# Attention and two dense layers on one core: one PSUM bank for the weighted values, seven common banks, and a new order from corrected durations

## The chip, the cores and the metric

The kernel runs on one core of a Trainium2 chip. Its engines are TensorE (PE, with its weight loads as PEld), VectorE (DVE), ScalarE (ACT), GpSimd (POOL) and SyncE (SP), which issues most transfers; each works through its own queue in order. TensorE writes into PSUM, which has eight banks here; DVE and ACT read it. The metric is the device time of one execution in microseconds: 618.28 us, median of three runs (617.89 to 619.36).

## What is computed

Inputs are q, k, v of shape (2, 8, 1152, 64) and the weights of two dense layers, all in 64-bit words that the kernel turns into pairs of 32-bit numbers (high and low part).

```python
q_pool = q.reshape(B, H, S // 2, 2, D).mean(axis=3)          # 576 queries a head
scores = scale * np.matmul(q_pool, k.transpose(0, 1, 3, 2))
scores = scores - np.max(scores, axis=-1, keepdims=True)
attn = np.exp(scores)
attn = attn / (np.sum(attn, axis=-1, keepdims=True) + 1e-09)
attn_out = np.matmul(attn, v)                                # as (1152, 512)
h = x @ w_in;  g = np.maximum(h, 0.0) + np.log1p(np.exp(-np.abs(h)));  x = g @ w_out
h = np.maximum(np.maximum(x @ w1, x @ w2), x @ w3);  out = h @ w_out2
```

## The kernel before

Two heads make a pair; there are eight pairs, and a pair's 576 queries are cut into units: three for pair 0 (128, 224 and 224 queries wide), two of 288 for each other pair, 17 units in all (`UNIT`). The keys come in nine tiles of 128. For a pair, q and k are loaded, transposed (`turn_q`, `turn_k`, the tiles `tq`, `tk`) and split into a high and a low part (`high_q`, `low_k`, ...). A first pass (`scores`, tile `s`, L908) multiplies the high parts alone, and DVE takes maxima from it (`part_max`, L921), which `spread` (tile `tm`) brings to all partitions.

A unit's main work is then, for each key tile j: `turned` (L956) makes transposed scores `st` from three products of high and low parts for two heads, into two banks; `exps` (L966) on ACT turns each into `p`; `add_p` (L975), on POOL, sums `p` into `acc`. `values` (L983) multiplies `p` with v for three key tiles at a time into the bank `x` of the unit; `x_6_1` below means the second such group of unit 6, `st_7_4` key tile 4 of unit 7. After the last key tile `sum_up` (L997) makes the row sum `l` in a common bank, and a chain follows: `keep_sum` (L1004), `log_sum` (L1010), `near_inverse` (L1014) on ACT, `inverse` in two steps (L1020, L1022) and `divide` (L1028) on DVE, which reads the bank `x` and writes the result `xy`.

TensorE works in three forms: row-split (two matmuls of 64 rows beside each other: `st`, `s`), column-split (64 columns: `x`, `l`, `tm`) and whole (the transposes).

The order of all this is written by a list scheduler (`Order.ordered`) when the program is built: each piece of work has an engine, a duration, a place (a wished time) and what it reads and writes; the engine that is free first takes the piece with the smallest place among those that could start. A change of TensorE's form costs `CHANGE` in it and `stay` in the place. Most PSUM results take a bank out of a pool `s` of common banks and give it back when their last reader is through (`take`, `free`): six in the kernel before, and two more for `x`, odd and even units apart. The places come from the table `AK`.

The first nine weights of the dense layers are rebuilt at low priority in the attention part (`early_float`, L259 to L272, and `low_weight`, L292, on DVE, with a common bank each). Then the dense part runs (`project`, L1213 in `matmul3`), with all eight banks under new names; its first matmul waits for the last reader of the bank that it gets.

Of the kernel before, what the change touches and what calls it, by code (L numbers as in the profile page):

```python
# [8 lines left out]
F32 = mybir.dt.float32  # L9
# [7 lines left out]
P = 128  # L17
# [13 lines left out]
SB = 448  # L31
BANK = 512

AK = {"load": 18.806, "load1": -361.956, "q1": 465.624, "k1": -601.474, "v0": -174.412, "p1": 16.097, "p2": -1.542, "kl": 95.048, "c0": -340.25, "v": 83.029, "q": -26.274, "k": -25.681, "pass": 2.655, "gap": 2.142, "values": 111.836, "sum": 55.437, "stay": 33.792}
WINDOW = 25.652
NPT = 20
ON_DVE = ((), (8,))
VALUES = ((0, 1, 2), (3, 4, 5), (6, 7, 8))
GOOD = 128 * 2 * 17
# [13 lines left out]
class Order:  # L53
# [1 line left out]

    CHANGE = {"rows": 0.21, "columns": 0.11, "whole": 0.15}
    AFTER = {"PE": 0.30, "ACT": 0.22, "DVE": 0.20, "POOL": 0.22, "SP": 2.6, "AQ": 2.6}

    def __init__(self, **pools):
# [87 lines left out]
def kernel(  # L149
# [22 lines left out]
    NJ = S // P  # L172
# [24 lines left out]
    ps = inner.enter_context(tc.tile_pool(name="ps", bufs=1, space=PSUM, side="right"))  # L197
# [110 lines left out]
    if exact:  # L308
        order = Order(t=NTB)
        tiles = {}  # L310
# [8 lines left out]
        for n in range(2):  # L319
            q1 = st.tile([P, 2, NQ + TAILQ], F32R, tag=f"q1{n}", name=f"q1_{n}")  # L320
# [415 lines left out]
        for n in range(NPRE + 3):  # L736
# [5 lines left out]
            if n < NPRE:  # L742
                for step in range(3):
                    order.add("DVE", (0.42, 0.65, 0.65)[step], late + 2 + step, float_weight, n, step,
                              reads=(f"raw{n % 3}", f"size{n % 2}"), writes=(f"t{n % 2}",))
# [3 lines left out]
            _, _, _, f, args, *_ = order.work[n]  # L749
            f(*args)  # L750
    else:
        order = Order(s=6)
        TRIO = 0.41
        order.mode = dict.fromkeys(("scores", "turned"), "rows") | dict.fromkeys(("values", "sum_up", "spread"), "columns")
        order.stay = AK["stay"]
        order.AFTER = {"PE": 0.20, "ACT": 0.16, "DVE": 0.14, "POOL": 0.10, "SP": 2.6}
        tiles = {}
        HQ = NQ // 2
# [166 lines left out]
        def step_of(u):  # L925
            return [w for w in range(UNITS) if UNIT[w][0] == UNIT[u][0]].index(u)
# [49 lines left out]

        def values(u, js):
            if js[0] == 0:
                tiles["x", u] = ps.tile([P, HQ], F32, tag=f"x{u % 2}", name=f"x_{u}")
            x, (pr, _, W) = tiles["x", u], UNIT[u]  # L980
            for j in js:
                for i in range(2):
                    nc.tensor.matmul(  # L983
                        x[halves(i), :W],
                        tiles["v", pr][:, i, j],
                        tiles["p", u, j][:, i, :W],
                        start=(j == 0),
                        stop=(j == NJ - 1),
                    )
# [60 lines left out]
        def name_of(n):  # L1050
            return f"b{n[1]}"
# [6 lines left out]
        def prepare_first():  # L1058
# [4 lines left out]
            for g, (t0, t1) in enumerate(q_parts(0)):  # L1063
# [3 lines left out]
                order.add("ACT", (0.21, 0.5)[g], p, high_q, 0, g, n, reads=(name_of(n),), writes=(f"qh0{g}",) if g else ("qh00", "qh01"))  # L1067
                order.add("DVE", (0.22, 0.55)[g], AK["c0"], low_q, 0, g, n, reads=(name_of(n), f"qh0{g}"), writes=(f"ql0{g}",), free=n)
            for g in range(NB):
                n, p = next_bank(), -55 + g  # L1070
                order.add("PE", 0.4, p, turn_k, 0, g, n, reads=(f"k{g}",), writes=(name_of(n),), take=n)
                order.add("ACT", 0.38, p, high_k, 0, g, n, reads=(name_of(n),), writes=[f"kh0{h}" for h in range(g, NB if g == 0 else g + 1)])
                order.add("DVE", 0.475, p + AK["kl"], low_k, 0, g, n, reads=(name_of(n), f"kh0{g}"), writes=(f"kl0{g}",), free=n)
            order.add("SP", 2.8, AK["v0"], load_v, 0, reads=(f"kh0{NB - 1}",), writes=("v0",))

        def prepare(pr):
            at, y = WINDOW * pr, pr % 2
            loads = AK["load1"] if pr == 1 else at + AK["load"]
            order.add("SP", 3.0, loads, load_q, pr, writes=("q", "q0"))
            order.add("SP", 3.0, loads + 0.1, load_k, pr, writes=["k"] + [f"k{g}" for g in range(NB)])  # L1080
            order.add("SP", 3.0, at + AK["v"], load_v, pr, reads=("k",), writes=(f"v{y}",))
            order.add(ADD_Q, 2.1 if ADD_Q == "POOL" else 1.3, (AK["q1"] if pr == 1 else at + AK["q"]) - 0.2, add_q, pr, reads=("q",), writes=("qs", "qs0"))
            for g in range(2):
                n, p = next_bank(), (AK["q1"] if pr == 1 else at + AK["q"]) + 0.5 * g
                order.add("PE", (0.24, 0.28)[g], p, turn_q, pr, g, n, reads=("qs",), writes=(name_of(n), f"tq{y}"), take=n)
                order.add("ACT", (0.38, 0.24)[g], p, high_q, pr, g, n, reads=(name_of(n),), writes=(f"qh{y}{g}",) if g else (f"qh{y}0", f"qh{y}1"))
                order.add("DVE", (0.47, 0.28)[g], p, low_q, pr, g, n, reads=(name_of(n), f"qh{y}{g}"), writes=(f"ql{y}{g}",), free=n)
            for g in range(NB):
                n, p = next_bank(), (AK["k1"] if pr == 1 else at + AK["k"]) + 0.5 * g
                order.add("PE", 0.28, p, turn_k, pr, g, n, reads=("k",), writes=(name_of(n), f"tk{y}"), take=n)  # L1090
                order.add("ACT", 0.38, p, high_k, pr, g, n, reads=(name_of(n),), writes=[f"kh{y}{h}" for h in range(g, NB if g == 0 else g + 1)])
                order.add("DVE", 0.475, p + AK["kl"], low_k, pr, g, n, reads=(name_of(n), f"kh{y}{g}"), writes=(f"kl{y}{g}",), free=n)

# [26 lines left out]
        def one_unit(u):  # L1120
            pr, c0, W = UNIT[u]
            y, part = pr % 2, W / HQ
            at, gap = WINDOW * pr + c0 / NQ * WINDOW, WINDOW / 2 / NJ * part
            for j in range(NJ):
                p, m = at + gap * j, u * NJ + j
                ns = [next_bank() for _ in range(2)]
                parts = range(1 if pr == 0 and step_of(u) == 0 else 2)
                order.add("PE", TRIO * max(part, 0.78), p, turned, u, j, *ns,
                          reads=[f"tq{y}", f"tk{y}"] + [f"{x}{y}{g}" for x in ("qh", "ql") for g in parts] + [f"{x}{y}{j // KT}" for x in ("kh", "kl")] + [f"nm{y}_{step_of(u)}"],
                          writes=[name_of(n) for n in ns], take=tuple(ns))  # L1130
                for i, n in enumerate(ns):
                    order.add("ACT", 0.09 + 0.23 * part, p, exps, u, j, n, i, reads=(name_of(n), f"shift{y}_{step_of(u)}"),
                              writes=(f"p{m % NPT}",), free=n)
                if j and j not in DIRECT:
                    engine = "DVE" if j in (ON_DVE[u % 2] if u + 1 < UNITS else LAST) else "POOL"
                    order.add(engine, 1.5 * part if engine == "POOL" else 0.96 * part, p, add_p, u, j, engine,
                              reads=[f"p{m % NPT}"] + ([f"p{(m - 1) % NPT}"] if j == 1 else []), writes=(f"acc{u % 2}",))
            for js in VALUES:
                p = at + gap * js[-1] + AK["values"] * part
                order.add("PE", 0.475 * len(js) * part, p, values, u, js,  # L1140
                          reads=[f"p{(u * NJ + j) % NPT}" for j in js] + [f"v{y}"], writes=(f"x{u % 2}",))
            n, p = next_bank(), at + gap * NJ + AK["sum"] * part
            order.add("PE", (0.475 + 0.475 * len(DIRECT)) * part, p, sum_up, u, n,
                      reads=[f"acc{u % 2}"] + [f"p{(u * NJ + j) % NPT}" for j in DIRECT], writes=(name_of(n),), take=n)
            r, x = f"rr{u % 2}", f"x{u % 2}"
            order.add("ACT", 0.58, p - 3, keep_sum, u, n, reads=(name_of(n),), writes=(r,))
            order.add("ACT", 0.34, p - 3, log_sum, u, writes=(r,))
            order.add("ACT", 0.53, p - 3, near_inverse, u, writes=(r,))
            order.add("DVE", 0.39, p - 3, inverse, u, 0, n, reads=(r,), writes=(name_of(n),))
            order.add("DVE", 0.39, p - 3, inverse, u, 1, n, reads=(name_of(n),), writes=(r,), free=n)  # L1150
            order.add("DVE", 0.39, p - 3, divide, u, reads=(r, x), writes=(f"xy{u}",))
            if (u + 1 == UNITS or UNIT[u + 1][0] != pr) and pr < NC:
                mine = [f"xy{w}" for w in range(UNITS) if UNIT[w][0] == pr]
                order.add("ACT", 0.45, p + 5, high_x, 0, pr, reads=mine, writes=(f"xh{pr}",))
                order.add("POOL", 1.08, p + 5, low_x, 0, pr, reads=(f"xh{pr}",))
# [16 lines left out]
        for n in range(NPRE + 3):  # L1172
# [5 lines left out]
            if n < NPRE:  # L1178
                t = next_bank()
                for step in range(3):  # L1180
                    order.add("DVE", 0.62, late + 2 if step == 0 else -100, early_float, n, step, t,
                              reads=(f"raw{n % 3}", f"size{n % 2}"), writes=(name_of(t),), take=None if step else t)
# [364 lines left out]
```

## Time and profile before

| | |
|---|---|
| median of three runs | 618.28 us (617.89 to 619.36) |
| the profiled execution | 618.21 us, span 616.4 us |
| TensorE's granted clock | 0.998 of full speed |
| first dense matmul | 252.94 us |
| PE busy in the span | 600.3 us (97%) |
| DVE, ACT, POOL busy | 407.1, 349.6, 366.8 us |

Times in rows are microseconds from the start of the span. A timeline row joins instructions of one group that follow each other: its first start, the time to the last end, and the count. Matmuls overlap in the pipe, so what a group takes from TensorE is read from its start to the next group's start, not from its length. A wait in brackets names what ended it.

### The profile page before, as it was taken

What the parts mean: (1) busy time and instruction counts of PE and PEld (TensorE: products, weight loads), DVE (VectorE), ACT (ScalarE), POOL (GpSimd) and SP (SyncE); (2) the same over time, 40 slices, a digit from 0 to 9 for tenths busy, and PEclk for the clock granted to TensorE, in tenths of its full rate; (3) what the DMA queues carried; (4) which work ended last, traced back from release to release, by engine and by line L of the source; (5) the groups of instructions that cost most, each with busy time, mean ns of one, the idle gap of its engine ahead of it and who ended that gap; (6) DMA issues with size and microseconds to landing.
All of it is one profiled execution on the core that took longest, in us unless ns stands there. A gap on an engine that the chain in (4) does not pass through costs nothing.

```text
span 616.4 us, 10975 instructions
## 1 busy us (share of the span) xinstructions
PE 600.3 (97%) x4116; PEld 512.3 (83%) x4116; DVE 407.1 (66%) x753; ACT 349.6 (57%) x817; POOL 366.8 (60%) x310
## 2 busy tenths in 40 slices
PE   7999999999999999999999999999999999999995
PEld 5866576666666566799999999999999999999994
DVE  5577667576779995789887988977888822212121
ACT  2656677776777779776777676766644312102101
POOL 1485787878888888499877878897946200000000
PEclk9999999999999999999999999999999999999999
DMA  6512131407042321133333333332234001001001
GB/s 154 154 41 85 33 93 24 116 2 208 13 112 70 107 79 61 34 104 104 102 109 117 117 104 103 102 103 70 68 103 138 35 1 52 0 1 53 0 1 56
DMA packets 53295, 46.68 MB, mean 76 GB/s; under 512 B 20592, under 2 KB 47216, under 8 KB 53232
## 3 DMA queue, kind: packets, MB, share of 16 engines
q1 hardware_dynamic: 51408, 45.29, 24.9%
q10 hardware_dynamic: 1824, 0.59, 0.4%
q8 instruction: 34, 0.56, 0.4%
q14 instruction: 29, 0.24, 0.1%
HBM read 43.52 MB, written 2.36 MB: 74 GB/s over the span
## 4 chain that ended last, share of the span: by engine, by line
PE 89%; DVE 5%; ACT 2%; POOL 1%; issue 1%; DMA 1%; SPq 0%; ACTq 0%; DVEq 0%; POOLq 0%
PE bank_h_m L1213 18%; PE bank_y L1213 16%; PE bank_h L1213 14%; PE st L956 12%; PE x L983 11%; PE bank_o L1213 6%; PE s L908 5%; PE l L997 2%; PE tk L881 2%; DVE nh L921 1%; ACT p L966 1%; DMA k<-in_k_dram 1%; PE tm L941 1%; PE tq L851 1%; DVE t L259 1%
## 5 line engine op out<-in xcount | busy, mean ns | idle before, releaser
L966 ACT ACTIVATE p<-st,shift 128x288 f32<-128x288 f32 (+2 forms) x306 | 127.3, 489 | 60.6 <-PE st L956 56.5
L975 POOL TENSOR_TENSOR acc<-acc,p 128x576 f32<-128x576 f32 (+2 forms) x96 | 128.2, 1335 | 15.6 <-ACT p L966 9.0
L921 DVE TENSOR_REDUCE nh<-s 128x1 f32<-128x512 f32 (+5 forms) x180 | 105.5, 631 | 40.5 <-PE s L908 40.0
L1213 PE MATMUL bank_h_m<-x,wh 128*128 128x384 f32 x432 | 114.1, 337 | 0.0
L1213 PE MATMUL bank_h<-x,wh 128*128 128x384 f32 x384 | 105.8, 338 | 1.9 <-DVE rr L1022 1.4
L248 POOL TENSOR_SCALAR size<-size 128x512 f32<-128x512 f32 x56 | 84.0, 1504 | 18.2 <-ACT size L243 18.1
L983 PE MATMUL x<-p,v 128*64 128x288 f32 (+2 forms) x612 | 81.5, 402 | 0.0
L1213 PEld LDWEIGHTS bank_h_m<-x,wh 128*128 128x128 f32 x432 | 78.7, 188 | 0.7
L1213 PE MATMUL bank_h_m<-x,wl 128*128 128x384 f32 x216 | 72.8, 337 | 0.0
L1213 PEld LDWEIGHTS bank_h<-x,wh 128*128 128x128 f32 x384 | 70.3, 188 | 2.8 <-issue 1.8
L956 PE MATMUL st<-qh,kh 64*128 64x288 f32 (+2 forms) x306 | 65.4, 351 | 1.7 <-DVE nh L921 1.0
L1268 POOL TENSOR_TENSOR d<-e,d 128x384 f32<-128x384 f32 x48 | 49.0, 1021 | 27.8 <-DVE d L1261 26.9
L1213 PE MATMUL bank_y<-gh,wh 128*128 128x384 f32 x192 | 65.2, 340 | 0.3 <-DVE gl L1292 0.3
L1213 PE MATMUL bank_y<-gh,wl 128*128 128x384 f32 x192 | 65.0, 339 | 0.0
L1213 PE MATMUL bank_y<-gl,wh 128*128 128x384 f32 x192 | 65.0, 339 | 0.0
L1213 PE MATMUL bank_h<-x,wl 128*128 128x384 f32 x192 | 64.8, 338 | 0.0
L983 PEld LDWEIGHTS x<-p,v 128*64 128x64 f32 x612 | 40.0, 138 | 26.8 <-issue 8.8
L956 PEld LDWEIGHTS st<-qh,kh 64*128 64x128 f32 x306 | 37.8, 193 | 27.1 <-ACT p L966 10.8
L956 PE MATMUL st<-ql,kh 64*128 64x288 f32 (+2 forms) x306 | 54.5, 308 | 0.0
L908 PE MATMUL s<-qh,kh 64*128 64x512 f32 (+3 forms) x306 | 51.1, 368 | 0.7 <-DVE nh L921 0.3
L956 PE MATMUL st<-qh,kl 64*128 64x288 f32 (+2 forms) x306 | 51.5, 297 | 0.0
L1277 POOL TENSOR_TENSOR d<-u,d 128x384 f32<-128x384 f32 x48 | 48.7, 1015 | 3.6
(219 smaller groups left out, 1097.7 us busy)
## 6 DMA issues: line engine op xcount, KB each, us to landing
raw<-in_moe_w_out_dram SPq DMA_DIRECT2D x22, 512.0 KB, 3.3
raw<-in_moe_w_dram SPq DMA_DIRECT2D x18, 512.0 KB, 3.5
raw<-in_moe_w_in_dram SPq DMA_DIRECT2D x16, 512.0 KB, 3.8
v<-in_v_dram SPq DMA_DIRECT2D x16, 288.0 KB, 3.6
k<-in_k_dram SPq DMA_DIRECT2D x14, 288.0 KB, 4.6
q<-in_q_dram SPq DMA_DIRECT2D x14, 256.0 KB, 3.4
out_dram<-ob SPq DMA_DIRECT2D x9, 256.0 KB, 2.8
qm<-in_q_dram SPq DMA_DIRECT2D x15, 32.0 KB, 4.0
```

Source lines behind the costliest of these rows:

```text
L248: nc.gpsimd.tensor_scalar(out=size, in0=size, scalar1=SMALLEST, scalar2=None, op0=ALU.max)
L881: nc.tensor.transpose(tp[:, t * P : (t + 1) * P], tiles["k", pr][:, g * KT + t].rearrange("p i d -> p (i d)"), ident)
L908: nc.tensor.matmul(tos[i][:, o * W : (o + 1) * W], kh[halves(i), j * P : (j + 1) * P], qh[halves(i), c0 : c0 + W], start=True, stop=True,)
L921: nc.vector.tensor_reduce(out=tiles["nh", pr][:, at : at + 1], in_=tiles[n][:, : W * len(some[x])], axis=AX.X, op=ALU.max, negate=True)
L956: nc.tensor.matmul(tos[i], key[halves(i), cols], query[halves(i), some], start=term == 0, stop=term == len(terms) - 1)
L966: nc.scalar.activation(out=tiles["p", u, j][:, i, :W], in_=tiles[n][:, :W], func=AF.Exp, bias=shift)
L975: engine.tensor_tensor(out=acc, in0=first, in1=tiles["p", u, j][:, :, :W], op=ALU.add)
L983: nc.tensor.matmul(x[halves(i), :W], tiles["v", pr][:, i, j], tiles["p", u, j][:, i, :W], start=(j == 0), stop=(j == NJ - 1),)
L997: nc.tensor.matmul(tiles[n][halves(i), :W], ones, part[:, i, :W], start=part is parts[0], stop=part is parts[-1])
L1213: nc.tensor.matmul(ps, lhs(a, kk), rhs(bb, kk), start=start and n == 0, stop=stop and n == last)
L1268: nc.gpsimd.tensor_tensor(out=d, in0=gs["e", i], in1=d, op=ALU.subtract)
L1277: nc.gpsimd.tensor_tensor(out=d, in0=gs["u", i], in1=d, op=ALU.add)
```

## The change

The pool of common banks has `8 - XB` banks, and `x` has `XB`, with `XB = 1`: so seven common banks, and one bank for the values of all units. In the scheduler's bookkeeping `x{u % XB}` is then one name, so the first `values` of a unit comes after the `divide` of the unit before. Durations in the list are altered (an exponential of 288 columns 0.385 instead of 0.32, the transposes 0.35, two steps of the chain shorter, `CHANGE` larger), and all places in `AK` are other numbers. No operation is added or taken away.

```diff
-AK = {"load": 18.806, "load1": -361.956, "q1": 465.624, "k1": -601.474, "v0": -174.412, "p1": 16.097, "p2": -1.542, "kl": 95.048, "c0": -340.25, "v": 83.029, "q": -26.274, "k": -25.681, "pass": 2.655, "gap": 2.142, "values": 111.836, "sum": 55.437, "stay": 33.792}
-WINDOW = 25.652
+AK = {"load": 10.098, "load1": -359.527, "q1": 470.177, "k1": -663.036, "v0": -197.836, "p1": 16.519, "p2": 0.036, "kl": 75.776, "c0": -330.331, "stay": 37.989, "v": 93.264, "q": -23.855, "k": -24.306, "pass": 3.391, "gap": 2.169, "values": 117.438, "sum": 51.809}
+WINDOW = 25.734
+XB = 1
-    CHANGE = {"rows": 0.21, "columns": 0.11, "whole": 0.15}
+    CHANGE = {"rows": 0.21, "columns": 0.17, "whole": 0.2}
-        order = Order(s=6)
+        order = Order(s=8 - XB)
-                tiles["x", u] = ps.tile([P, HQ], F32, tag=f"x{u % 2}", name=f"x_{u}")
+                tiles["x", u] = ps.tile([P, HQ], F32, tag=f"x{u % XB}", name=f"x_{u}")
-                order.add("PE", 0.28, p, turn_k, pr, g, n, reads=("k",), writes=(name_of(n), f"tk{y}"), take=n)
+                order.add("PE", 0.35, p, turn_k, pr, g, n, reads=("k",), writes=(name_of(n), f"tk{y}"), take=n)
-                    order.add("ACT", 0.09 + 0.23 * part, p, exps, u, j, n, i, reads=(name_of(n), f"shift{y}_{step_of(u)}"),
+                    order.add("ACT", 0.2 + 0.185 * part, p, exps, u, j, n, i, reads=(name_of(n), f"shift{y}_{step_of(u)}"),
-                          reads=[f"p{(u * NJ + j) % NPT}" for j in js] + [f"v{y}"], writes=(f"x{u % 2}",))
+                          reads=[f"p{(u * NJ + j) % NPT}" for j in js] + [f"v{y}"], writes=(f"x{u % XB}",))
-            r, x = f"rr{u % 2}", f"x{u % 2}"
-            order.add("ACT", 0.58, p - 3, keep_sum, u, n, reads=(name_of(n),), writes=(r,))
+            r, x = f"rr{u % 2}", f"x{u % XB}"
+            order.add("ACT", 0.45, p - 3, keep_sum, u, n, reads=(name_of(n),), writes=(r,))
-            order.add("ACT", 0.53, p - 3, near_inverse, u, writes=(r,))
+            order.add("ACT", 0.4, p - 3, near_inverse, u, writes=(r,))
```

TensorE around the sum of unit 6, one row of each group, in the order before (unit 6's last values `x_6` with `p_6_6`, unit 7's first `x_7` with `p_7_0`):

```order
L983 MATMUL x_6_1575<-p_6_6_1626,v_2_896 64x288 x2
...
L956 MATMUL st_7_3_0_1777<-qh_3_1276,kh_3_1290 128x288
...
L908 MATMUL s_4_0_1_0_1785<-qh_4_1696,kh_4_1709 128x512
...
L956 MATMUL st_7_4_0_1792<-qh_3_1276,kh_3_1290 128x288
...
L983 MATMUL x_7_1802<-p_7_0_1690,v_3_1394 64x288 x2
...
L997 MATMUL l_6_1843<-acc_6_1533,ones_102 64x288
```

and in the order after:

```order
L998 MATMUL l_6_1788<-acc_6_1529,ones_102 64x288
...
L957 MATMUL st_7_5_0_1805<-qh_3_1318,kh_3_1311 128x288
...
L909 MATMUL s_4_0_2_0_1816<-qh_4_1738,kh_4_1731 128x512
...
L984 MATMUL x_6_1605<-p_6_6_1614,v_2_1022 64x288 x2
...
L957 MATMUL st_7_6_0_1835<-qh_3_1318,kh_3_1311 128x288
...
L909 MATMUL s_4_0_3_0_1848<-qh_4_1738,kh_4_1731 128x512
...
L957 MATMUL st_7_7_0_1855<-qh_3_1318,kh_3_1311 128x288
...
L984 MATMUL x_7_1865<-p_7_0_1690,v_3_1424 64x288 x2
```

The sum of unit 6 has moved from behind the first values of unit 7 to ahead of the last values of its own unit, and six groups stand between it and the first values of unit 7.

VectorE at the same chain (inverse, inverse, `divide` of unit 6; `nh` are maxima), before:

```order
L1020 SCALAR_TENSOR_TENSOR l_6_1843<-l_6_1843,rr_6_1856 128x288
L1022 SCALAR_TENSOR_TENSOR rr_6_1856<-l_6_1843,rr_6_1856 128x288
L921 TENSOR_REDUCE nh_4_1756<-s_4_0_4_0_1880 128x1
...
L921 TENSOR_REDUCE nh_4_1756<-s_4_0_5_1_1912 128x1
L1028 SCALAR_TENSOR_TENSOR xy_99<-x_6_1575,rr_6_1856 128x288
```

and after:

```order
L1021 SCALAR_TENSOR_TENSOR l_6_1788<-l_6_1788,rr_6_1813 128x288
L1023 SCALAR_TENSOR_TENSOR rr_6_1813<-l_6_1788,rr_6_1813 128x288
L1029 SCALAR_TENSOR_TENSOR xy_99<-x_6_1605,rr_6_1813 128x288
L922 TENSOR_REDUCE nh_4_1778<-s_4_0_3_0_1848 128x1
L922 TENSOR_REDUCE nh_4_1778<-s_4_0_3_1_1849 128x1
```

The `divide` has moved ahead of the maxima. VectorE at the end of the attention part, after (`t_7`, `wl_7` and the like are weights 7 and 8):

```order
L1021 SCALAR_TENSOR_TENSOR l_15_3643<-l_15_3643,rr_15_3689 128x288
L1023 SCALAR_TENSOR_TENSOR rr_15_3689<-l_15_3643,rr_15_3689 128x288
L260 TENSOR_SCALAR t_7_3708<-size_7_3360 128x512
L269 SCALAR_TENSOR_TENSOR t_7_3708<-raw_7_3289,t_7_3708 128x512
L273 SCALAR_TENSOR_TENSOR t_7_3708<-raw_7_3289,t_7_3708 128x512
L1029 SCALAR_TENSOR_TENSOR xy_99<-x_15_3676,rr_15_3689 128x288
L260 TENSOR_SCALAR t_8_3722<-size_8_3564 128x512
L269 SCALAR_TENSOR_TENSOR t_8_3722<-raw_8_3349,t_8_3722 128x512
L293 TENSOR_TENSOR wl_7_3725<-t_7_3708,wh_7_3724 128x512
L273 SCALAR_TENSOR_TENSOR t_8_3722<-raw_8_3349,t_8_3722 128x512
L1021 SCALAR_TENSOR_TENSOR l_16_3711<-l_16_3711,rr_16_3718 128x288
```

Before, the inverse and `divide` of units 15 and 16 stood there together, with no weight between them.

## Rows read from the trace of the kernel before

**Rows 1.** The page's chain that ended last, share of the span by engine.
```profile
PE 89%; DVE 5%; ACT 2%; POOL 1%; issue 1%; DMA 1%; SPq 0%; ACTq 0%; DVEq 0%; POOLq 0%
```

**Rows 2.** Stretches: us, length, then busy us of PE, PEld, DVE, ACT, POOL; clock; DMA.
```profile
56.00:81.60 25.60, 25.20 (x225) 16.46 (x223) 17.13 (x33) 18.17 (x48) 19.11 (x14) 1.00 0.27 70
...
109.90:138.00 28.10, 27.86 (x256) 18.46 (x255) 18.90 (x37) 20.22 (x53) 22.33 (x18) 1.00 0.26 64
...
166.30:196.40 30.10, 29.56 (x262) 19.25 (x261) 25.28 (x48) 22.66 (x57) 26.89 (x21) 1.00 0.28 75
196.40:226.00 29.60, 28.66 (x238) 18.31 (x239) 28.42 (x53) 23.74 (x60) 24.82 (x19) 1.00 0.36 110
226.00:252.90 26.90, 25.41 (x236) 16.18 (x232) 15.92 (x27) 22.73 (x60) 18.09 (x13) 1.00 0.13 40
252.90:609.80 356.90, 356.01 (x1964) 347.33 (x1964) 227.10 (x403) 172.78 (x358) 182.84 (x161) 1.00 0.22 70
```

**Rows 3.** Weight loads' waits before 253 us: who for whom, us in total, times, longest.
```profile
PEld st L956 <- ACT p L966: 10.8, 34, 0.4
...
PEld s L908 <- ACT p L966: 6.8, 21, 0.4
PEld st L956 <- DVE nh L921: 5.5, 14, 0.5
```

**Rows 4.** Timeline of PE: start us, us, engine, line, operation, out<-in, count.
```profile
121.36 0.30 PE L956 MATMUL st<-qh,kh 64*128 64x288 f32 x2
...
121.85 1.68 PE L983 MATMUL x<-p,v 128*64 128x288 f32 x12
123.45 0.50 PE L908 MATMUL s<-qh,kh 64*128 64x512 f32 x2
123.79 0.29 PE L956 MATMUL st<-qh,kh 64*128 64x288 f32 x2
...
124.19 0.72 PE L956 MATMUL st<-qh,kh 64*128 64x288 f32 x2
...
125.00 0.55 PE L908 MATMUL s<-qh,kh 64*128 64x512 f32 x2
...
127.08 0.40 PE L956 MATMUL st<-qh,kh 64*128 64x288 f32 x2
...
127.58 0.41 PE L908 MATMUL s<-qh,kh 64*128 64x512 f32 x2
127.80 0.31 PE L956 MATMUL st<-qh,kh 64*128 64x288 f32 x2
```

**Rows 5.** Timeline of PE, an x group between two spreads.
```profile
225.41 1.62 PE L983 MATMUL x<-p,v 128*64 128x288 f32 x12
226.87 0.39 PE L941 MATMUL tm<-ident,nm 128*64 128x128 f32 x4
```

**Rows 6.** Timeline of ACT, the chain of unit 6.
```profile
121.13 0.50 ACT L1004 ACTIVATE rr<-l,tiny 128x288 f32<-128x288 f32 x1
...
122.11 0.88 ACT L966 ACTIVATE p<-st,shift 128x288 f32<-128x288 f32 x2
122.87 0.44 ACT L1014 ACTIVATE rr<-rr 128x288 f32<-128x288 f32 x1
```

**Rows 7.** Timeline of DVE, the chain of unit 6.
```profile
123.94 0.46 DVE L1022 SCALAR_TENSOR_TENSOR rr<-l,rr 128x288 f32<-128x288 f32 x1
124.31 2.50 DVE L921 TENSOR_REDUCE nh<-s 128x1 f32<-128x512 f32 x4
126.73 0.45 DVE L1028 SCALAR_TENSOR_TENSOR xy<-x,rr 128x288 f32<-128x288 f32 x1
```

**Rows 8.** Timeline of DVE, then PE, where the dense part begins.
```profile
252.34 0.46 DVE L1022 SCALAR_TENSOR_TENSOR rr<-l,rr 128x288 f32<-128x288 f32 x1
...
252.94 0.41 PE L1213 MATMUL bank_h<-x,wh 128*128 128x384 f32 x1 [1.35 <-DVE rr L1022]
```

**Rows 9.** Groups of DVE from 166.3 to 226: busy us, mean ns, idle before.
```profile
L259 DVE TENSOR_SCALAR t<-size 128x512 int32<-128x512 int32 x7 | 4.8, 685 | 0.3 <-ACT p L966 0.3
```

More of the change, by code (lines that the diff above doesn't have):

```diff
@@ L1084, in prepare @@
                 n, p = next_bank(), (AK["q1"] if pr == 1 else at + AK["q"]) + 0.5 * g
-                order.add("PE", (0.24, 0.28)[g], p, turn_q, pr, g, n, reads=("qs",), writes=(name_of(n), f"tq{y}"), take=n)
+                order.add("PE", 0.35, p, turn_q, pr, g, n, reads=("qs",), writes=(name_of(n), f"tq{y}"), take=n)
                 order.add("ACT", (0.38, 0.24)[g], p, high_q, pr, g, n, reads=(name_of(n),), writes=(f"qh{y}{g}",) if g else (f"qh{y}0", f"qh{y}1"))
```

## The prediction

> **What bounds the kernel now.** I read the chain of waits first. It is TensorE for 89% [rows 1]: any gain has to shorten TensorE's own queue. The stretches come next [rows 2]: from 252.9 us to 609.8 TensorE is busy 356.0 of 356.9 us. That is the dense part, whose order the change leaves nearly as it is, so nothing can be won there. The attention part ends at 252.9. The page calls TensorE busy there too, but it counts matmuls that stand in the pipe, so I went to starts. In the row-split form one `st` group (six matmuls) takes 0.40 us to the next start (123.79 to 124.19), one `s` group 0.22 (127.58 to 127.80) [rows 4]; an `x` group (three key tiles) with column-split work on both sides takes 1.46 (225.41 to 226.87) [rows 5]. Whatever exceeds these is either a change of form or a wait:
>
> - Changes of form: the last `st` ahead of an `x` takes 0.49 (121.36 to 121.85), the `x` ahead of an `s` 1.60 (to 123.45), the first `st` behind an `x` 0.50 (127.08 to 127.58) [rows 4]. Leaving rows costs 0.09, leaving columns 0.15, entering rows 0.10. In the same way entering the whole-array transposes costs about 0.05 and leaving them 0.09.
> - Waits: the second `st` of the pair at 124.19 takes 0.81 instead of 0.40 [rows 4]. The list of waits names them: weight loads of `st` and `s` stood 10.8 and 6.8 us for the exponentials on ScalarE, and `st` 5.5 us for the row maxima on VectorE [rows 3]. Those are the instructions that release common PSUM banks. ScalarE is busy 20.2 of 28.1 us in a window of two units, GpSimd 22.3, VectorE 18.9 [rows 2], so the waits are bursts that six banks cannot absorb; no engine lacks the time over a whole window.
>
> One such window (109.9 to 138.0, one of three alike) adds up so: 18 `st` at 0.40, 9 `s` at 0.22, 6 `x` at 1.46 make 18.0; two row sums, the two short score ends, two spreads and five transposes some 5.1 by their starts; 19 changes of form 3.2. Of 28.1 us, 1.8 are left as waits. The same sum for the other stretches leaves 4.0 (56 to 81.6), 2.0, 1.8, 2.0, 2.8 (166.3 to 196.4), 5.9 (196.4 to 226), and 2.2 to the end, 1.4 of them the wait of the first dense matmul for the last inverse [rows 8]. Before 56 us the same sum leaves about 17, most of them the arrival of the inputs and the short first units.
>
> The profiled execution took 618.21 us, 1.8 more than its span of 616.4; the median of the three runs is 618.28, so the sum is made against 618.2.
>
> **The change part by part.** No instruction is added or removed; the matmul groups are the same 368, in another order, with other banks.
>
> *Changes of form.* I counted the borders in the two orders of the attention part. Before: rows to columns 66, columns to rows 71, rows to whole 9, whole to rows 4, whole to columns 6, together 156. After: 62, 62, 5, 5, 6, and 5 from columns straight to whole, together 145. With the costs above: 66 x 0.09 + 71 x 0.25 + 9 x 0.14 + 4 x 0.19 + 6 x 0.14 = 26.6 before; 5.6 + 15.5 + 0.7 + 1.0 + 0.8 and 5 x 0.20 = 24.6 after. Columns to whole does not occur before; 0.20 is its two halves, 0.14 to 0.25 the nearest rows, which moves the sum by 0.3. Term: **-2.0 us**.
>
> *A seventh common bank and corrected durations.* The list had charged 0.32 us for an exponential of 288 columns. In the trace the first of two starts 0.38 before the second (two in 122.11 to 122.87) [rows 6]; the new figure is 0.385. So the old order put `st` groups closer than ScalarE could release them; the new one knows it, and has a seventh bank. I followed one new window with the durations above. From `x_8_0` on, six `st` and two short `s` stand without an `x` among them: 3.5 us of TensorE, 4.6 us of ScalarE; seven banks hold three pairs, and the delay comes out at about 0.3 us where before it was 1.0. The second half leaves 0.1 to 0.3. So I put 0.6 a window for bank waits in place of 1.9: -1.3 for each of three windows, and from the less regular neighbours (4.0 and 2.8) to 2.0 each, -2.8. Together -6.7. Bounds: 0, if the waits only move, and -12.6, if all go.
>
> *One bank for the values.* Now the first `x` of a unit waits for `divide` of the unit before. Queued behind it on TensorE is everything, since the queue is in order. The chain before: `keep_sum` starts at 121.13, at the end of the sum, then come `log_sum`, two exponentials, `near_inverse` at 122.87 [rows 6], the second inverse 123.94, which lasts 0.46 [rows 7]; a `divide` directly behind it ends 3.8 us after the sum. In the new order VectorE has it directly behind for units 3 to 11 (before, four maxima stood between, and it started at 126.73 [rows 7]). On TensorE, between `l_6` and the first `x_7`, stand `st`, `s`, `x`, `st`, `s`, `st`: 0.50 + 0.34 + 1.60 + 0.50 + 0.23 + 0.49 = 3.7. Against 3.8 and the signal to TensorE, which took 0.14 at the first dense matmul (inverse done at 252.34 + 0.46, start at 252.94 [rows 8]), about 0.3 us of wait. Between `l_7` and `x_8` stand 4.3 us: none. So **+0.3 us in each of four windows, +1.2**. Bounds: 0 and 2.5 a unit, the latter if `divide` comes as late as at 126.73.
>
> *The late part (166 to 253).* VectorE is busy 25.3 of 30.1 and 28.4 of 29.6 us there [rows 2], since the first nine weights are rebuilt. That work stays. Between `l_12` and `l_13` the new order has seven `st` and five `s` and no `x`; with 0.61 us for each maximum (four from 124.31 to 126.73 [rows 7]) and seven banks I get 2.4 us of wait, and 0.3 more for `divide` of unit 12. Before, the same stretch had 5.9 in all. I take -1.7.
>
> *The end.* Before: 1.4 for the last chain. Now `l_16` stands ahead of all three `x_16`, so its chain hides behind 4.4 us of values. But VectorE has the three steps of a weight (0.69 us each [rows 9]) between the last inverse and the `divide` of unit 15, on which `x_16` waits: about 1.3. Term **-0.1**.
>
> *The opening.* Other order, same inputs: 0, with 2 us either way.
>
> Sum: -2.0 - 6.7 + 1.2 - 1.7 - 0.1 = -9.3. My walk through two windows sees only the waits that I looked for, and each order has small ones. I keep the counted -2.0 and +1.2, and two thirds of the other 8.5, -5.7: **-6.5**, so 611.7.
>
> **The rivals.**
>
> *A. One bank for the values costs more than it gives.* The place: units 11 to 14, where VectorE is fullest; there maxima and weight steps stand around the chain, and `i1_12` and `dv_12` are six maxima apart. Price: 2.5 us of lateness as above at four handovers, 10 us, against the 6.5 saved: 618.2 - 6.5 + 10 = 621.7. It decides from 6.5 us of stalls in all. For it: the 126.73. Against it: in the new order nine `divide`s stand directly behind their inverses, and around unit 12 other TensorE work was put between.
> The Trainium skill's page Perfetto Trace Analysis (Matmuls) says that independent matmul groups should rotate through different banks, so that emptying one overlaps the next group. The values of successive units no longer do. If nothing overlapped, each of 16 handovers would cost the 0.45 of a `divide` and the signal, 0.6, again 10 us and 621.7. The rows speak for partial cover only, 3.7 of 3.9 us; the chance stands with A.
>
> *B. The banks were not it.* ScalarE and GpSimd feed the sums and `p` tiles at their own pace, the waits come back at other places, only the changes of form remain, less the handovers: 618.2 - 2.0 + 1.2 = 617.4. For it: GpSimd at 22.3 of 28.1. Against: the waits name bank releases, and ScalarE idles 8 us a window.
>
> *C. The gain in full*, with a good opening: 618.2 - 9.3 - 2 = 606.9.
>
> **How the numbers follow.** Forecast (608.5 to 615.5) 0.50; C and beyond 0.15; B 0.21; A 0.14. The range reaches from C to the dearer side of B: 606.5 to 619. A measurement of this kernel can tell 0.3%, 1.9 us, so faster is under 616.4. Forecast and C give 0.65, a third of B 0.07: faster 0.72. The rest of B and a little of A: same 0.15. Most of A: slower 0.13.
>
> **What would show it.** Right: the first dense matmul near 246 us instead of 252.9 and the same 357 us from there on; three alike windows of about 26.8 to 27.4 us; `st` after `st` at 0.40 without the 0.81; weight loads of `st` and `s` waiting for the exponentials well under 10.8 and 6.8. The step on the handover is right if the first `x` of units 5, 7, 9, 11 shows a wait for `xy` of some 0.3, and wrong at over 1. The step on the end is right if `x_16` waits about 1.3 for `divide`. The whole is wrong if the windows stay at 28, or if the dense part gets longer.

## The result, and the profile after

| | before | after |
|---|---|---|
| median, us | 618.29 (617.89 to 619.36) | 604.99 (604.0 to 605.28) |
| ratio | 1 | 0.9782 (95%: 0.9769 to 0.9796) |
| span of the profiled execution, us | 616.4 | 603.1 |
| first matmul of the dense part, us | 252.94 | 239.72 |
| dense part, us | 356.9 | 356.9 |

The change makes the kernel 13.3 us faster, twice the forecast of 6.5 and below the range. Line numbers of the changed kernel are those of before plus one. One of the four runs of bank and places, a kernel further down, took 618.5 us at a lower granted clock (0.983) and is left out of the figures for it.

The chain of the page, which answers to [rows 1]:

```profile
PE 88%; ACT 4%; DVE 3%; POOL 1%; issue 1%; DMA 1%; ACTq 0%; SPq 0%; DVEq 0%
```

Stretches of the changed kernel, columns as in [rows 2]:

```profile
51.00:78.00 27.00, 27.00 (x284) 18.99 (x282) 18.52 (x39) 20.45 (x56) 20.74 (x15) 1.00 0.24 67
105.05:132.05 27.00, 26.66 (x256) 17.74 (x254) 18.64 (x37) 19.94 (x53) 22.40 (x17) 1.00 0.25 67
...
186.55:212.90 26.35, 26.20 (x228) 17.15 (x228) 25.99 (x50) 22.53 (x57) 24.26 (x18) 1.00 0.32 104
212.90:239.72 26.82, 25.44 (x243) 16.30 (x239) 19.04 (x31) 22.36 (x59) 16.87 (x13) 1.00 0.16 50
239.72:596.60 356.88, 356.02 (x1966) 347.28 (x1964) 225.46 (x403) 174.25 (x360) 184.89 (x162) 1.00 0.22 71
```

TensorE is still the path. The window of two units is 27.00 us long where 28.1 stood in [rows 2], with the same 256 matmuls, and the dense part is the same to 0.02 us. All of the gain lies ahead of it.

Who the weight loads of the attention part wait for (0 to 240 us; us in total, times, longest), answering to [rows 3]:

```profile
PEld st L957 <- DVE nh L922: 6.7, 17, 0.4
...
PEld s L909 <- ACT p L967: 6.0, 17, 0.4
PEld x L984 <- DVE xy L1029: 5.0, 10, 1.9
PEld st L957 <- ACT p L967: 4.2, 14, 0.4
```

`st` waits 4.2 us for exponentials in place of 10.8; `s` hardly less than before (6.0 against 6.8), and the maxima hold `st` a little longer (6.7 against 5.5). New is `x` waiting for the `divide` (`xy`) of the unit before. These sums are idle time of the weight loads, which run beside the matmuls, and do not measure what TensorE loses. The kernel with the bank alone, described below, shows it: its `st` loads wait as long as before for the exponentials, and it is 6.0 us faster.

```profile
PEld st L957 <- ACT p L967: 10.7, 29, 1.0
```

So I summed TensorE's time from start to start with the prices of the prediction (the work of each group, each change of form) in every kernel; what is over is waiting. In us, between landmarks that every order has (a pair stands for the start of its transposes, "list on six banks" for durations and places without the seventh bank, described below):

| stretch | before | after | bank alone | list on six banks |
|---|---|---|---|---|
| to the transposes of pair 2 | 17.2 | 16.9 | 18.4 | 25.0 |
| pair 2 to pair 3 | 3.9 | 0.3 | 1.6 | 3.1 |
| three alike windows, pairs 3 to 6 | 5.8 | 2.7 | 1.8 | 9.6 |
| pair 6 to pair 7 | 2.7 | 2.2 | 2.6 | 4.8 |
| pair 7 to the sum of unit 15 | 6.8 | 3.1 | 4.5 | 7.8 |
| from there to the dense part | 1.5 | 1.7 | 3.8 | 0.1 |
| changes of form (count) | 26.7 (156) | 24.7 (145) | 25.5 (150) | 25.0 (145) |

### The profile page after: what moved, and what is told of

It reads as the page before. It is cut to its first block, busy times and chain, and to the rows that moved or that the text cites. A ratio compares the mean times of both kernels' runs of the same rounds, so it can differ in the third digit from the quotient of the medians.

```text
span 603.1 us, 10994 instructions
## 1 busy us (share of the span) xinstructions
PE 588.0 (98%) x4116; PEld 507.6 (84%) x4116; DVE 404.1 (67%) x753; ACT 349.8 (58%) x817; POOL 367.3 (61%) x310
## 3 DMA queue, kind: packets, MB, share of 16 engines
q1 hardware_dynamic: 51408, 45.29, 24.9%
## 4 chain that ended last, share of the span: by engine, by line
PE 88%; ACT 4%; DVE 3%; POOL 1%; issue 1%; DMA 1%; ACTq 0%; SPq 0%; DVEq 0%
PE bank_h_m L1214 19%; PE bank_y L1214 16%; PE bank_h L1214 15%; PE st L957 11%; PE x L984 10%; PE bank_o L1214 6%; PE s L909 5%; PE l L998 3%; ACT p L967 2%; PE tk L882 2%; PE tm L942 1%; DVE nh L922 1%; PE tq L852 1%; ACT rr L1005 1%; DMA k<-in_k_dram 1%
## 5 line engine op out<-in xcount | busy, mean ns | idle before, releaser
L967 ACT ACTIVATE p<-st,shift 128x288 f32<-128x288 f32 (+2 forms) x306 | 125.8, 499 | 46.2 <-PE st L957 43.2
L922 DVE TENSOR_REDUCE nh<-s 128x1 f32<-128x512 f32 (+5 forms) x180 | 104.2, 630 | 26.7 <-PE s L909 26.0
L1269 POOL TENSOR_TENSOR d<-e,d 128x384 f32<-128x384 f32 x48 | 49.1, 1023 | 25.5 <-DVE d L1262 24.2
L957 PE MATMUL st<-qh,kh 64*128 64x288 f32 (+2 forms) x306 | 59.5, 347 | 0.7
L957 PEld LDWEIGHTS st<-qh,kh 64*128 64x128 f32 x306 | 35.0, 193 | 21.5 <-DVE nh L922 6.7
L957 PE MATMUL st<-ql,kh 64*128 64x288 f32 (+2 forms) x306 | 51.3, 303 | 0.0
L1331 DVE TENSOR_TENSOR mg<-bank_h_m,mg 128x384 f32<-128x384 f32 x18 | 10.0, 555 | 61.6 <-PE bank_h_m L1214 61.6
L957 PE MATMUL st<-qh,kl 64*128 64x288 f32 (+2 forms) x306 | 49.7, 297 | 0.0
```

The source lines that it names most:

```text
L922: nc.vector.tensor_reduce(out=tiles["nh", pr][:, at : at + 1], in_=tiles[n][:, : W * len(some[x])], axis=AX.X, op=ALU.max, negate=True)
L957: nc.tensor.matmul(tos[i], key[halves(i), cols], query[halves(i), some], start=term == 0, stop=term == len(terms) - 1)
L967: nc.scalar.activation(out=tiles["p", u, j][:, i, :W], in_=tiles[n][:, :W], func=AF.Exp, bias=shift)
L1269: nc.gpsimd.tensor_tensor(out=d, in0=gs["e", i], in1=d, op=ALU.subtract)
```

## The experiments

**The parts of the change one by one.** The list's two parts (durations; places) and the seventh bank, each alone and two together. Three theories were on record for the first four runs; the expectations name them.

The bank alone (old durations, old places):

```diff
+XB = 1
-        order = Order(s=6)
+        order = Order(s=8 - XB)
...
```

> The kernel before with seven common banks and one bank for the values; durations and places as before. The list then writes an order with 150 changes of form (25.4 us by the prediction's prices, against 26.6 before and 24.6 after). Theory 1, the banks: the seventh bank takes up the bursts of ScalarE and VectorE whatever the places are; 608 to 611 us, the three alike windows at 27.2 to 27.6. Theory 2, the list: banks help only an order whose durations and places fit the chip; 614 to 620, windows at 27.8 to 28.5 us. Theory 3, it takes all of them together: 616 or more.

The durations alone, two banks of values and six common:

```diff
+XB = 2
-                    order.add("ACT", 0.09 + 0.23 * part, p, exps, u, j, n, i, ...
+                    order.add("ACT", 0.2 + 0.185 * part, p, exps, u, j, n, i, ...
...
```

> The kernel before with the corrected durations alone; banks and places as before, 158 changes of form. Theory 1: 616 to 619 us. Theory 2: the list now knows that an exponential takes 0.385 us and puts other work between; 611 to 615. Theory 3: 616 or more, since the places were found for the old durations.

The places alone, six common banks:

```diff
+XB = 2
-WINDOW = 25.652
+WINDOW = 25.734
...
```

> The kernel before with the new places alone; banks and durations as before, 140 changes of form, 2.8 us less by the prediction's prices. Theory 1: 615 to 617 us, the changes of form alone. Theory 2: 613 to 617. Theory 3: 616 or more.

Durations and places without the bank (the changed kernel with one number other):

```diff
-XB = 1
+XB = 2
```

> The changed kernel with two banks for the values and six common ones (XB = 2); its durations and places kept, 146 changes of form. Theory 1: most of the gain is lost, 613 to 616 us, and the weight loads wait for the exponentials as before (10 us and 7 us). Theory 2: most of the gain stays, 606 to 610 us; the first values of units 5, 7, 9, 11 then don't wait for the divide. Theory 3: 614 to 618.

The changed kernel with one part of the list taken back, first the places (bank and durations), then the durations (bank and places):

```diff
-WINDOW = 25.734
+WINDOW = 25.652
...
```

> Seven common banks and one bank of weighted values, with the corrected durations, but with the places of the kernel before. Theory P (the new places are what the seventh bank needs; durations alone only move the order within a place): 611 to 613 us, as with the bank alone (612.3), since the durations alone gave +2.1 on six banks. Theory D (the durations give the second half of the gain once a seventh bank is there): 605 to 608 us. The form changes of the order are 151, so forms give -0.9 us against the kernel before in both.

```diff
-                    order.add("ACT", 0.2 + 0.185 * part, p, exps, u, j, n, i, ...
+                    order.add("ACT", 0.09 + 0.23 * part, p, exps, u, j, n, i, ...
...
```

> Seven common banks and one bank of weighted values, with the new places, but with the old durations. Theory P: the new places give most of the second half of the gain: 605 to 609 us. Theory D: without the durations the new places are worth little: 611 us or more. Third possibility, that the two numbers fit only each other: over 612.3, so slower than the bank alone. The form changes are 150 (145 in the changed kernel), so 0.8 us of the distance to 605.0 belong to the forms.

Measured, us (ratio to the kernel before, 95%):

| | six common banks | seven |
|---|---|---|
| old list | 618.3 | 612.30 (0.9896 to 0.9929) |
| durations | 620.19 (1.0025 to 1.0060) | 620.11 (1.0029 to 1.0063) |
| places | 632.34 (1.0219 to 1.0261) | 610.29 (0.9856 to 0.9934) |
| both | 629.92 (1.0178 to 1.0214) | 604.99 (0.9769 to 0.9796) |

The bank alone gives 6.0 us. The list writes a new order when the number of banks changes, so this is the bank together with the order that follows from it (1.2 us of it are changes of form, 25.5 for 26.7); the old order itself with seven banks was not run. No part of the list gives anything clear of the noise by itself: on six banks it costs 2 to 14 us, and with seven banks the places are not clear of the bank alone (610.3 with runs from 609.0 to 614.2, against 612.3), while the durations take the bank's gain back. Both halves with the seventh bank give a further 7.3 over the bank alone. Of the three theories the third, that it works only all together, holds for the list and not for the bank, and no theory had both halves on six banks at over 618, where 629.9 was measured. The two that shared the second half of the gain out between places and durations both fell: durations with the bank were expected at 611 to 613 or at 605 to 608 and took 620.1.

**Why the list loses without the rest.** Stretches of the places alone, columns as in [rows 2], the second of them nearly all at half the clock:

```profile
34.50:43.50 9.00, 7.85 (x21) 3.58 (x20) 9.00 (x16) 0.00 (x0) 1.32 (x2) 0.81 0.23 66
39.60:46.40 6.80, 6.55 (x29) 4.20 (x30) 5.65 (x13) 1.46 (x4) 1.54 (x2) 0.53 0.00 0
```

VectorE in the same kernel, then the weight loads beside it:

```profile
34.47 9.06 DVE L922 TENSOR_REDUCE nh<-s 128x1 f32<-128x512 f32 x16
```

```profile
36.41 0.18 PEld L909 LDWEIGHTS s<-qh,kh 64*128 64x128 f32 x1 [0.42 <-DVE nh L922]
37.01 0.18 PEld L909 LDWEIGHTS s<-qh,kh 64*128 64x128 f32 x1 [0.41 <-DVE nh L922]
```

And VectorE in the changed kernel:

```profile
34.79 4.87 DVE L922 TENSOR_REDUCE nh<-s 128x1 f32<-128x512 f32 x8
40.24 2.65 DVE L922 TENSOR_REDUCE nh<-s 128x1 f32<-128x512 f32 x4 [0.58 <-PE s L909]
43.76 3.68 DVE L922 TENSOR_REDUCE nh<-s 128x1 f32<-128x512 f32 x6 [0.87 <-PE s L909]
```

With the places alone sixteen maxima of pair 1 stand in one row, and with them the score matmuls. Each of these waits for the bank that a maximum gives back, every 0.60 us; TensorE has 0.18 us of loads in each 0.60, ScalarE has nothing at all, and from 40.0 us TensorE's granted clock is at the lower level, 1.2 GHz, for 6.8 us. With both parts of the list and six banks it is the same row of 16 and 10.2 us at that level (what the lower clock costs stands as waiting in the table above). In the changed kernel the rows are 8, 4 and 6 with other work between, and the clock stays at 1.00.

Seven banks with the durations have a row of 16 too, so the row does not go with the number of banks alone. Its maxima, and four stretches of that kernel (columns as in [rows 2]):

```profile
41.42 9.86 DVE L922 TENSOR_REDUCE nh<-s 128x1 f32<-128x512 f32 x16 [0.43 <-PE s L909]
```

```profile
45.10:51.90 6.80, 6.79 (x31) 3.53 (x30) 6.24 (x11) 0.95 (x3) 0.68 (x1) 0.50 0.01 2
55.40:58.70 3.30, 3.30 (x23) 2.30 (x19) 1.74 (x6) 2.32 (x6) 0.97 (x2) 0.50 0.00 0
191.90:195.20 3.30, 3.30 (x28) 2.71 (x26) 2.90 (x8) 2.15 (x7) 3.22 (x3) 0.50 0.31 108
243.10:246.40 3.30, 2.90 (x12) 1.50 (x14) 3.16 (x8) 1.32 (x6) 0.00 (x0) 0.50 0.00 0
```

TensorE is at the lower level for some 17 us there, two of the four stretches far behind the opening. At half speed that is at most 8.5 us, as much as the whole 7.8 by which this kernel is behind the bank alone; so its 620.1 us do not show that the durations harm the order by anything but the clock and the row.

To see whether this opening is the loss, I shortened these maxima alone. The edit takes the maxima of pair 1 over 64 columns and leaves out the rest:

```diff
-                in_=tiles[n][:, : W * len(some[x])], axis=AX.X
+                in_=tiles[n][:, : 64 if pr == 1 else W * len(some[x])], axis=AX.X
```

> The new places alone (632.3 us, six common banks), with the maxima of pair 1 taken over 64 of up to 512 columns (its shifts are then not the true maxima, and the output not the reference's); the order is the same. Theory O (the loss sits in the opening: 16 maxima of 0.57 us in a row feed TensorE a fifth of the time, and it then runs at half clock for 6.8 us): no stretch at half clock, and 622 to 625 us, that is 8 to 10 us less: some 5 of waits and 3.4 of clock. Theory W (the loss is spread over the later windows, whose waits are 3.2 us each in place of 2.0): 629 us or more. The rest over 618 is then the later windows in either case.

> Seven banks with the corrected durations (620.1 us), the maxima of pair 1 over 64 columns as well. Theory O: no stretch at half clock before 60 us, and 610 to 613 us, so the durations would be worth nothing by themselves and lose only by the opening. Theory W: 617 us or more.

> Seven banks with the new places (612.2 us, runs from 609.0 up), the maxima of pair 1 over 64 columns as well. Theory O: no stretch at half clock before 60 us, and 603 to 607 us, near the changed kernel. Theory W: 609 us or more.

> The control: the changed kernel (605.0 us) with the maxima of pair 1 over 64 columns. It has no stretch at half clock to lose; its maxima of pair 1 stand in rows of 8, 4 and 4. Theory O: 602 to 604.5 us, a gain of 0.5 to 3. If it gains as much as the other three, the shorter maxima themselves are the gain and not the row and the clock.

| short maxima of pair 1 in | us | without them |
|---|---|---|
| places alone | 624.15 (623.17 to 624.79) | 632.34 |
| bank and durations | 614.61 (612.27 to 615.8) | 620.11 |
| bank and places | 611.36 (609.49 to 613.36) | 610.29 |
| the changed kernel | 604.53 (603.65 to 604.74) | 604.99 |

The same stretches of the places alone, with short maxima:

```profile
34.50:43.50 9.00, 9.00 (x92) 7.18 (x88) 3.67 (x22) 4.23 (x13) 5.53 (x6) 1.00 0.23 67
39.60:46.40 6.80, 6.80 (x80) 5.23 (x78) 0.29 (x1) 5.21 (x16) 5.35 (x6) 1.00 0.02 5
```

In 9 us TensorE runs 92 matmuls in place of 21, and the clock is 1.00. So the opening is 8.2 of the 14 us that the places lose alone, and 5.5 of the 7.8 by which the durations spoil the bank. With the places alone, 6.8 us at half speed are at most 3.4 of that and the rest is the row itself; the short maxima take away both, so no run separates them. The control gains 0.5, inside the spread of its runs, so short maxima are no gain by themselves. The theory missed for bank and places: 603 to 607 expected, 611.4 measured, no gain; with short maxima its waits from pair 6 to the dense part are still 10.2 us where the changed kernel has 7.0. Why that pairing places its late groups worse was not tried further and stays open. The other 6 us that the places lose alone lie later. The three alike windows have 9.6 us of wait, with short maxima and with long, where the kernel before has 5.8; with short maxima the two stretches from pair 6 to the sum of unit 15 have 16.5 by the same sum, where it has 9.5. The changes of form (2.7 us less) and the end (1.4 less) give a part of this back.

**The late waits of the kernel before.** Are they VectorE's rebuilding of weights, or banks?

```diff
-            float_weight(n, step)
+            float_weight(n, step, 64 if step else None)
...
```

The second and third step then work on 64 of 512 columns and leave the rest of the weight unbuilt.

> The kernel before, with the second and third of VectorE's steps of the nine early weights done on 64 of their 512 columns (the rest of these weights is left unbuilt, so its output isn't the reference's); the order of every engine is the same. It takes about 0.5 us from each of 18 steps. Theory V (the late waits of the kernel before, 6.8 us between the transposes of pair 7 and the sums of unit 15, come from these steps standing ahead of what TensorE waits for): those waits fall by 3 us or more, and the time to 613 us or less. Theory B (they come from the six common banks, since every kernel with seven has 1.0 us or less before the sums of unit 15 and every one with six has 3.0 or more): these late waits stay within 1 us, and the time falls by 0 to 1.5 us.

617.23 us (0.9966 to 0.9988). The waits from pair 7 to the sum of unit 15 go from 6.8 to 6.1, so these steps are not what most of them come from. That it is the banks is shown for a part: the bank alone takes the waits to 4.5. Every kernel with seven banks and full steps has at most 1.1 us in the second half of that stretch (units 13 to 15), every one with six at least 3.0.

**The end of the attention part.** TensorE and VectorE there, changed kernel:

```profile
228.21 4.59 PE L984 MATMUL x<-p,v 128*64 128x288 f32 x36
232.63 0.71 PE L998 MATMUL l<-acc,ones 128*64 128x288 f32 x4
...
235.20 4.59 PE L984 MATMUL x<-p,v 128*64 128x288 f32 x36 [1.38 <-DVE xy L1029]
239.72 0.45 PE L1214 MATMUL bank_h<-x,wh 128*128 128x384 f32 x1
```

```profile
232.26 0.46 DVE L1023 SCALAR_TENSOR_TENSOR rr<-l,rr 128x288 f32<-128x288 f32 x1
232.64 0.68 DVE L260 TENSOR_SCALAR t<-size 128x512 int32<-128x512 int32 x1
...
234.09 0.70 DVE L273 SCALAR_TENSOR_TENSOR t<-raw,t 128x512 int32<-128x512 int32 x1
234.70 0.45 DVE L1029 SCALAR_TENSOR_TENSOR xy<-x,rr 128x288 f32<-128x288 f32 x1
```

These answer to [rows 8]: the wait for the last inverse is gone, and one of 1.38 us for the `divide` of unit 15, behind three weight steps, is there. Two kernels try to take it away: the `divide` first, and then also other banks for the first dense matmuls.

```diff
-                              reads=(f"raw{n % 3}", f"size{n % 2}"), ...
+                              reads=(f"raw{n % 3}", f"size{n % 2}") + ((f"xy{UNITS - 2}",) if n >= NPRE - 2 else ()), ...
```

> The changed kernel, with VectorE's divide of unit 15 ahead of the steps of the last two early weights; TensorE's order is the same. x of unit 16 waited 1.6 us for that divide. Theory G (that wait is on the path and nothing is late behind it): -1.6 us, 603.4. Theory N (the first dense matmul needs a bank that the rebuilt weight 8 and the end of the units free, and takes over the wait): no gain, within 0.5 us of 605.0, with the first dense matmul at 239.5 to 240.2 us as it is now (239.72).

```diff
-    FIRST = (4, 5, 6, 7, 2, 3, 1)
+    FIRST = (5, 6, 2, 3, 1, 7, 4)
```

> As end_divide_first, and the dense part takes its banks in another order (5, 6, 2, 3, 1, 7, 4 instead of 4, 5, 6, 7, 2, 3, 1), so that its first matmuls stand in banks that were read early. Theory N: the wait that the first kernel only moved goes: 603.0 to 603.8 us, first dense matmul at 238.1 to 238.6. Theory of no use (the dense part's own transfers or weights set its end): within 0.5 us of 605.0 although its first matmul is earlier.

The `divide` first: 604.96 us (0.9773 to 0.9806), no gain, as theory N has it; `x_16` starts at 234.11, but the first dense matmul at 240.47, behind VectorE's `wl`:

```profile
240.47 0.44 PE L1214 MATMUL bank_h<-x,wh 128*128 128x384 f32 x1 [1.78 <-DVE wl L293]
```

With the free bank: 604.8 us (0.9777 to 0.9809). The first dense matmul stands at 237.96, 1.76 earlier than in the changed kernel, and still nothing is won:

```profile
237.96 0.44 PE L1214 MATMUL bank_h<-x,wh 128*128 128x384 f32 x1
```

Waits from 234 to 270 us, the changed kernel and then this one:

```profile
PEld bank_y L1214 <- DVE gl L1293: 1.3, 2, 0.9
```

```profile
PEld bank_y L1214 <- DVE gl L1293: 2.4, 2, 2.0
```

The dense part's second product takes back 1.1 us of it: it needs gate values from VectorE, which still has the weights to build. (By the 255th weight load of that part the two kernels stand 0.24 us apart.) Whether VectorE limits this end is tested by the same steps made short in the changed kernel:

> The changed kernel with the same 18 VectorE steps on 64 of 512 columns (again weights are left unbuilt). Theory E (what is left over at the end of the units is VectorE: the wait of x of unit 16 for the divide of unit 15, 1.6 us, and then the first gate values that the dense part's second product waits for): the first dense matmul 1.4 to 2 us earlier, and, other than in the kernel with the free bank, the gain stays: 602.5 to 603.7 us. Theory of no use: the gain is taken back in the dense part as there, 604.3 us or more.

603.44 us (603.1 to 604.28; ratio 0.9741 to 0.9774): 1.5 us kept.

```profile
231.50 0.71 PE L1002 MATMUL l<-acc,ones 128*64 128x288 f32 x4
...
233.17 4.59 PE L988 MATMUL x<-p,v 128*64 128x288 f32 x36 [0.48 <-DVE xy L1033]
237.68 0.45 PE L1218 MATMUL bank_h<-x,wh 128*128 128x384 f32 x1
```

The first dense matmul stands 2.0 us earlier than in the changed kernel. Of these, 1.1 are there at the sum of unit 16 already (231.50 against 232.63); the end itself gives the 0.9 by which `x_16` waits less for the `divide`, and the dense part takes back none of the 2.0 up to its last weight load. So VectorE's steps limit this end. The kernel leaves out work and is no version to use. No version tried computes the whole and beats the changed kernel by more than the noise.

**The price of a change of form.** One matmul more behind each of 102 blocks of the changed kernel's dense part:

```diff
+        nc.tensor.matmul(scratch[:64, :P], ident[:, :64], ident, start=True, stop=True)
...
```

`scratch` is a bank of its own, so that the dense part of both kernels here has six banks in place of seven.

> The changed kernel with one more matmul of 128 columns behind each of 102 blocks of the dense part, into a bank of its own that nobody reads (so the dense part has six banks), its weights 64 columns wide: TensorE goes from the whole array to columns and back 102 times. Against its twin with weights 128 columns wide. The prediction's prices (0.14 into columns, 0.20 back): 35 us more than the twin. If a change of form costs nothing of its own (the sums of waits then hold them): under 5 us more.

and its twin, with `ident[:, :P]` into the whole of `scratch`:

> The twin: the same 102 matmuls of 128 columns with weights 128 columns wide, so that TensorE stays in the whole form. 102 by about 0.11 us (128 columns; 384 take 0.338) make 11 us more than the changed kernel, 616, and a little more if the dense part misses its seventh bank.

661.55 and 629.85 us: 31.7 us over 102 pairs of changes, 0.31 each; the prediction had 0.34. Weight loads of the added matmuls, to columns and then whole (us, mean ns, idle before):

```profile
L1244 PEld LDWEIGHTS scratch<-ident 128*64 128x64 f32 x204 | 19.5, 134 | 25.6 <-issue 25.6
```

```profile
L1244 PEld LDWEIGHTS scratch<-ident 128*128 128x128 f32 x204 | 37.0, 189 | 0.0
```

Most of the price shows as idle "issue" time of the weight loads, a wait for nothing that the profile names, 0.25 us a pair of changes. The page TensorEngine Tiling (Array Packing) of the Trainium skill (Key Properties) says that a change of mode drains TensorE. That a round trip costs 0.31 us agrees with it. The twin alone cost 24.9 us more than the changed kernel and not 11: each such matmul is two instructions (204 loads in the rows), which the expectation forgot. Two times 11 leave about 2.5 us, which may be the bank that the dense part gave up; no run separates this.

## Why the prediction was half the size

Right, by their own rows:

- *What bounds it*: the dense part did not move (356.88 us), the gain is in TensorE's waits and forms before it.
- *Changes of form*: the count stands. Of the prices a run tested one kind, the whole array to columns and back (0.31 for 0.34); taken for all kinds, that would make the term -1.8 in place of -2.0. Rows to columns and back, the most frequent kind, is priced from the starts alone.
- *The three alike windows*: 27.00 us, inside 26.8 to 27.4. Waits went from 5.8 to 2.7, -3.1; the uncut terms said -3.9 and +0.9.
- *Handover*: 0.3 us of wait was promised at the first `x` of units 5, 7, 9 and 11. TensorE stands idle there 0.28 to 0.29 us each, 1.1 in all for the 1.2 of the sum, and at the first `x` of no other unit but the last. The row of unit 7, with the `st` ahead at 0.83 to the next start:

```profile
113.93 0.30 PE L957 MATMUL st<-qh,kh 64*128 64x288 f32 x2
...
114.76 1.68 PE L984 MATMUL x<-p,v 128*64 128x288 f32 x12 [0.28 <-DVE xy L1029]
```

- The page Perfetto Trace Analysis of the Trainium skill (Matmuls) advises rotating banks between independent groups. The row agrees that a handover without it costs something, 0.28 us here, but what the freed bank gave was more: 6.0 us with the old list.
- *The end*: `x_16` waits 1.38 us by the row for 1.3 expected. *The opening*: 16.9 against 17.2.

Partly right: the waits of `st` loads for exponentials fell well, from 10.8 to 4.2; those of `s` were to be well under 6.8 and are 6.0. As a sign of the bank the first is worth little, since the bank alone leaves it at 10.7.

Wrong, and this is the step that failed: **the cut at the end, "two thirds of the other 8.5", and two terms too small.** The uncut sum was -9.3. The cut took 2.8 us from it because a walk through windows might miss small waits of the new order. The sum of waits shows none missed where I had walked. The other part is size:

| term | predicted | measured |
|---|---|---|
| pair 2 to pair 3 (56 to 81.6) | -2.0 | -3.6 |
| pair 7 to the sum of unit 15 | -1.7 | -3.7 |
| all others, uncut | -5.6 | -5.7 |
| the cut | +2.8 | 0 |

(Of the others, predicted and measured: forms -2.0 and -2.0, the three windows with their handovers -3.0 and -3.1, pair 6 to pair 7 -0.5 and -0.5, the opening 0 and -0.3, the end -0.1 and +0.2.) In the first stretch I took "less regular" as a reason to leave 2.0 us of the 4.0. In the late one I left 4.2 of 5.9 (counted to 226 us; to the sum of unit 15 it is 6.8) and blamed VectorE's weight steps for what would stay; with those steps short the kernel before keeps 6.1 of 6.8 us. The walk between the sums of units 12 and 13 was right, 2.4 us of wait by it and about as much by the sum of starts. What I had not walked was the rest up to the sum of unit 15, where over 3 us of wait go to under 1. In each of the two stretches the bank alone takes 2.3 us out, the list another 1.3 and 1.4.

Rival A (one bank of values costs more than it gives) and B (banks were not it) are both refuted by the bank alone, 612.3. Rival C, 606.9, was nearest: its gain in full came, the 2 us that it counted on from the opening did not (0.3).

That the forecast of 6.5 matches what the bank gives alone, 6.0, is chance: the terms were worked out on the new order. What I had not seen is that the list's worth depends on the bank by 18.9 us (+11.6 without it, -7.3 with it), nor that the opening of an order could run at half the clock. Both numbers hold what the row and the clock cost in the orders that have them.

## What to carry to other kernels

When waits have been followed one by one and the sum is in hand, don't cut it by a share for unknowns; put the unknown into the range, and treat the irregular stretches with the same walk as the regular ones. An order and the number of buffers that it was laid out for are one edit: here the list costs 11.6 us without its bank and gives 7.3 with it, so the loss of a part tested alone says nothing against the whole. And look what stands in a row on a slow engine while the fast one waits for it: here the row cost once as waits and, by at most 3.4 us with the places alone, again in the clock.

## What was not expected of the hardware

- TensorE's granted clock fell to its lower level for 6.8 to 10.2 us in rows of score matmuls that came one per 0.60 us, in three orders, at times when the changed kernel and the kernel before stay at 1.00. With the row shortened it stayed up there. It also fell for 3.4 us at other places: at 204.6 us with the durations alone, at 55.3, 191.9 and 243.1 with bank and durations, and with short maxima at 212.3 (places alone) and 235.3 (bank and durations). No run tried what brought these about.
- Going from the whole array to column form and back costs 0.31 us, and most of it shows only as "issue" idle of the weight loads (25.6 us over 204 loads, of 31.7).
